# A masked copy of float64 bits in a compact tile, with its engine chosen by a list scheduler, and reordered first loads, in a one-core attention and feed-forward kernel

## The chip, the cores and the metric

One core of one Trainium2 chip. The metric is the device time of one execution in microseconds; lower is better. The kernel before has been run three times, and one further execution was taken with the profiler.

## What is computed

The inputs are float64 arrays for the weights and float32 for q, k, v. Three parts follow each other:

```python
kv  = einsum('bhsd,bhse->bhde', k, v)          # 8 batches, 8 heads, 576 rows, 64 wide
out = einsum('bhsd,bhde->bhse', q, kv)
x   = out / sqrt(mean(out * out, -1) + 1e-6) * g_norm      # then laid out as 4608 x 512
h   = maximum(maximum(x @ w1, x @ w2), x @ w3)             # 512 -> 768
x1  = h @ w_out                                            # 768 -> 512
g   = s * relu(x1 @ w_in) ** 2 + b                         # 512 -> 2048
y   = g @ w_out2                                           # 2048 -> 512
```

## The kernel before, in words

The rows are handled in nine blocks of 512 columns: one for each batch, and a ninth that gathers the 64 left-over rows of all eight batches. A product is kept near float32 accuracy by splitting each operand into a high and a low part and making three matmuls of 128x128 by 128x512 for each step (`mm3`, lines 154 to 157). The second feed-forward layer runs after all nine blocks, in stages that the change does not touch; only its weights are converted ("p" tiles, 32 of them) while the blocks are running.

**Weights.** They arrive as float64 bits and are turned into float32 on the core. `conv_load` (line 219) loads a tile of 128x512 numbers as 16-bit words, four to a number, into the slot that the finished weight will have (`W1S[n]` or `WOS[m]`). Then, in `plan_conv` (line 552): `conv_c` (line 235) clears the sign of the top word of each number and writes it into the fourth word of the same number, in place, that is at a step of 8 bytes; `conv_t` (line 253) makes the exponent and upper mantissa from it on ScalarE; `conv_r` (line 241) makes the low mantissa bits; `conv_s` (line 249) adds the sign; `conv_sum` (line 257) joins the two; `conv_hi` and `conv_lo` split the result. For the weights of the first layer ("w" tiles, 18, and "o" tiles, 6) `conv_c` runs on ScalarE, and `conv_r` on ScalarE for odd tiles and on VectorE for even ones; for "p" tiles both run on VectorE.

**Order of work.** Every step of the nine blocks is a `job` with a position, an engine, an estimated cost, and the names that it reads and writes. `arrange` (line 73) is a list scheduler: it simulates the engines with these costs and always starts the job that can begin first, among those on one engine the one with the lowest position. The order that comes out is then fixed for each engine: the engines run their instructions in that order, each waiting for what it needs, and nothing behind a waiting instruction on the same engine passes it. SyncE issues all loads and stores in this way (its queue is SPq in the rows).

**The start.** Positions count one per weight tile of 12 matmuls; a block takes 22 (`SL`), and the work ahead of block 0 begins at `Z = -12`. Batch 0: q is loaded, turned by TensorE and copied out; for each of four head pairs p, k and v are loaded, multiplied (`kv_mm`, line 322, including the left-over rows "rem"), copied (`kv_out`), and used (`o_mm`, line 389). For each two pairs a chain of small steps follows: copy out (line 409), square (415), mean over the heads by matmul (441), three ScalarE steps (451, 453, 455), two VectorE steps (457, 459), broadcast by matmul (470), scaling (475), and the split into xh (275) and xl (278). Call these chain 1 (pairs 0 and 1) and chain 2 (pairs 2 and 3). Weight tiles 0 to 3 are used pair by pair as they come: three matmuls for each tile and pair, 48 in all. From then on `g1_part` (line 509) makes 12 matmuls per tile, `g2_mm` (536) the 72 of the second product, while batch 1 goes through its attention (`plan_o`, `plan_norm`).

**Loads around the change.** Weight tiles 0 to 3 are loaded at positions `Z + LP[n]` with `LP = (3.35, 3.65, 3.95, 4.25)`, behind most of batch 0's q, k and v; the later tiles at `0.85 n - 5`, the "o" tiles at `10 + 0.8 m`; batch 2's k, v at 6, 9, 12, 15, its left-over rows at 6.01, its q at 12. The load of left-over rows of one batch has to wait until the products of the batch before have read the old ones. "o" tiles 4 and 5 share their slots with working tiles of the "w" conversions.

```python
def conv_c(key, eng):
    if eng == "ACT":
        act(out=mag16(key).bitcast(BF16), in_=top16(key).bitcast(BF16), func=AF.Abs)
    else:
        ts(out=mag16(key), in0=top16(key), scalar1=0x7FFF, scalar2=None, op0=ALU.bitwise_and)
```

## Time and profile before

| | us |
|---|---|
| three runs, median (lowest to highest) | 1410.27 (1410.04 to 1412.35) |
| the profiled execution, its own time | 1408.85 |
| its span, first to last instruction | 1406.8 |
| TensorE busy in the span | 1375.7 |
| VectorE busy | 909.9 |
| ScalarE busy | 750.5 |

The busy time of TensorE is the time in which at least one matmul was under way; matmuls overlap, so one that is shown with 0.39 us follows its neighbour after less. A row of the timeline gives the start, the duration, engine, line and shapes, and in brackets the idle time of the engine just before, with what ended it. In the rows, PE is TensorE, PEld its weight loads, DVE VectorE, ACT ScalarE, POOL GpSimd and SPq the queue of SyncE that issues transfers.

### The profile page before, as it was taken

The page shows a single profiled execution, that of the slowest core. Times are in us where ns is not written, and L with a number is a line of the kernel's source. Part 1 is how long each engine was busy: PE and PEld are TensorE (multiplying, and loading weights), DVE is VectorE, ACT ScalarE, POOL GpSimd, SP SyncE. Part 2 cuts the span into 40 slices and gives each one's busy share as a digit, 9 for nine tenths or more (in the row PEclk, how much of TensorE's full clock was granted, in tenths as well). Part 3 has the DMA queues.
Part 4 walks back from the last instruction along what each step waited for, and adds up shares of the span by engine and source line. Part 5 has one row for each costly group of instructions (what it writes and reads, how often), then busy time and mean ns, then how long its engine had stood idle before and what let it go on. Part 6 is the DMA issues. An engine that isn't in the chain of part 4 may idle for free. (4 is left out here: it accounts for less than half of the span.)

```text
span 1406.8 us, 19559 instructions
## 1 busy us (share of the span) xinstructions
PE 1375.7 (98%) x7056; PEld 1124.4 (80%) x7056; DVE 909.9 (65%) x1434; ACT 750.5 (53%) x1299; POOL 237.3 (17%) x175
## 2 busy tenths in 40 slices
PE   6999999999999999999999999999999999999997
PEld 3677888888888878888888789887888888888887
DVE  3886646465645462444648757467877978888884
ACT  6895434343424342333557456556775656566565
POOL 0000222221213132212000000000002314141412
PEclk9899999999999999999999999999999999999999
DMA  9976364445546320030354735544685454544441
GB/s 264 280 134 144 77 179 87 145 99 161 83 128 115 98 69 35 1 120 0 120 209 159 244 149 194 180 163 156 200 302 157 146 198 150 173 151 150 155 143 38
DMA packets 221328, 202.51 MB, mean 144 GB/s; under 512 B 117168, under 2 KB 175536, under 8 KB 219056
## 3 DMA queue, kind: packets, MB, share of 16 engines
q1 hardware_dynamic: 221072, 201.02, 48.0%
q8 instruction: 55, 0.90, 0.3%
q14 instruction: 41, 0.34, 0.1%
q10 hardware_dynamic: 160, 0.26, 0.0%
HBM read 126.79 MB, written 74.45 MB: 143 GB/s over the span
## 5 line engine op out<-in xcount | busy, mean ns | idle before, releaser
L155 PE MATMUL g<-xh,w_w 128*128 128x512 f32 x648 | 257.0, 397 | 4.1 <-ACT w_w L275 4.1
L157 PE MATMUL g<-xh,w_w 128*128 128x512 f32 x648 | 254.3, 393 | 0.2 <-DVE w_w L278 0.2
L156 PE MATMUL g<-xl,w_w 128*128 128x512 f32 x648 | 254.0, 392 | 0.0
L151 ACT ACTIVATE zx<-z 128x512 fp32r<-128x512 f32 (+1 forms) x280 | 161.2, 587 | 123.1 <-PE zs_a L963 34.0
L885 PE MATMUL ps_a<-x_q,w_q 128*128 128x512 f32 (+1 forms) x960 | 209.9, 370 | 3.5 <-DVE cs L793 3.2
L963 PE MATMUL zs_a<-zx,w_q 128*128 128x512 f32 (+1 forms) x960 | 203.8, 369 | 0.5 <-POOL zx L152 0.3
L885 PEld LDWEIGHTS ps_a<-x_q,w_q 128*128 128x128 f32 x960 | 167.4, 188 | 37.1 <-DVE cs L793 5.3
L152 DVE TENSOR_TENSOR zx<-z,zx 128x512 fp32r<-128x512 f32 (+1 forms) x234 | 172.5, 755 | 35.1 <-ACT zx L151 34.7
L963 PEld LDWEIGHTS zs_a<-zx,w_q 128*128 128x128 f32 x960 | 167.9, 188 | 32.0 <-POOL zx L152 0.7
L152 POOL TENSOR_TENSOR zx<-z,zx 128x512 fp32r<-128x512 f32 (+1 forms) x46 | 64.4, 1400 | 591.0 <-DMA gd<-cs 379.7
L527 DVE TENSOR_TENSOR h<-g,h 128x512 f32<-128x512 f32 x108 | 74.6, 691 | 115.4 <-PE g L157 114.0
L155 PEld LDWEIGHTS g<-xh,w_w 128*128 128x128 f32 x648 | 122.4, 189 | 33.1 <-ACT w_w L275 6.4
L157 PEld LDWEIGHTS g<-xh,w_w 128*128 128x128 f32 x648 | 122.5, 189 | 27.9 <-DVE w_w L278 2.0
L156 PEld LDWEIGHTS g<-xl,w_w 128*128 128x128 f32 x648 | 122.7, 189 | 25.3
L278 POOL TENSOR_TENSOR h<-h,h 128x512 fp32r<-128x512 f32 x40 | 54.7, 1367 | 464.2 <-ACT h L275 464.2
L885 PE MATMUL ps_b<-x_q,w_q 128*128 128x512 f32 (+1 forms) x480 | 106.4, 369 | 1.4 <-ACT cs L896 1.1
L963 PE MATMUL zs_b<-zx,w_q 128*128 128x512 f32 (+1 forms) x480 | 103.8, 371 | 1.9 <-DVE zx L152 1.9
L275 ACT ACTIVATE h<-h 128x512 fp32r<-128x512 f32 x54 | 34.1, 631 | 131.1 <-DVE h L527 130.6
L963 PEld LDWEIGHTS zs_b<-zx,w_q 128*128 128x128 f32 x480 | 83.9, 188 | 18.9 <-DVE zx L152 3.2
L885 PEld LDWEIGHTS ps_b<-x_q,w_q 128*128 128x128 f32 x480 | 83.9, 188 | 17.9 <-ACT cs L896 1.9
L155 PE MATMUL g<-h,w_o 128*128 128x512 f32 x216 | 84.7, 392 | 0.3 <-DVE h L527 0.3
L156 PE MATMUL g<-h,w_o 128*128 128x512 f32 x216 | 84.1, 389 | 0.0
(171 smaller groups left out, 2009.5 us busy)
## 6 DMA issues: line engine op xcount, KB each, us to landing
z<-gd SPq DMA_DIRECT2D x64, 512.0 KB
gd<-cs SPq DMA_DIRECT2D x96, 256.0 KB
z<-gd SPq DMA_DIRECT2D x48, 256.0 KB
x1d<-x SPq DMA_DIRECT2D x36, 256.0 KB
raw_w<-in_moe_w_dram SPq DMA_DIRECT2D x18, 511.0 KB
k<-in_k_dram SPq DMA_DIRECT2D x32, 256.0 KB
v<-in_v_dram SPq DMA_DIRECT2D x32, 256.0 KB
wd<-tr_p SPq DMA_DIRECT2D x32, 256.0 KB
```

The lines of the kernel that those rows point to most:

```text
L151: act(out=hi, in_=src, func=AF.Copy)
L152: eng.tensor_tensor(out=lo, in0=src, in1=hi.bitcast(F32), op=ALU.subtract)
L155: nc.tensor.matmul(ps, lhsT=w[:, 0, sl], rhs=xh, start=first, stop=False)
L156: nc.tensor.matmul(ps, lhsT=w[:, 0, sl], rhs=xl, start=False, stop=False)
L157: nc.tensor.matmul(ps, lhsT=w[:, 1, sl], rhs=xh, start=False, stop=last)
L275: act(out=out, in_=src, func=AF.Copy)
L278: eng.tensor_tensor(out=out, in0=src, in1=hi.bitcast(F32), op=ALU.subtract)
L527: nc.vector.tensor_tensor(out=st["h", m], in0=ps, in1=st["h", m], op=ALU.max)
L885: nc.tensor.matmul(ps, lhsT=w[:, a, c], rhs=x[:, b_], start=new and k == 0 and e == 0, stop=k == HK - 1 and e == 2, skip_group_check=True)
L963: nc.tensor.matmul(ps, lhsT=w[:, a, c], rhs=x[:, b_, :n], start=new and k_ == 0 and e == 0, stop=k_ == 3 and e == 2, skip_group_check=True)
```

## The change

A mask's result goes into a compact tile of its own ("gc", 128x512 16-bit numbers, two buffers) instead of back between the float64 words. The list scheduler can be given two engines for one job with a cost for each; it takes the one that can begin first, the cheaper one at a tie. `conv_c` and `conv_r` of all tiles are given so. Weight tile 0 is loaded ahead of everything else (`LP[0] = -1`), tiles 1 to 3 take the positions that 0 to 2 had. Batch 2's k, v, left-over rows and q are placed behind the "o" tiles (14.5 to 17). Some estimated costs of loads change. Batch 1's attention is placed one position earlier and its norm steps closer together. `WS_`, `WO_`, `KM`, `AS`, `K1`, `KS` and `QP` carry the values that stood in the code before.

```diff
-    SIZE = {"g": 4, "t": 2, "st": 2, "qt": 2, "o": 2, "kvc": 3, "k": NP, "v": NP}
+    SIZE = {"g": 4, "t": 2, "st": 2, "qt": 2, "o": 2, "kvc": 3, "k": NP, "v": NP, "cgc": 2}
...
     def job(pos, eng, cost, fn, *args, r=(), w=(), a=(), lag=None):
-        jobs.append((pos, len(jobs), eng, cost, fn, args, r, w, a, lag or (2.0 if eng == "SP" else 0.1)))
+        jobs.append((pos, len(jobs), eng, cost, fn, list(args), r, w, a, lag or (2.0 if eng == "SP" else 0.1)))
...
             if not need[n]:
-                heaps.setdefault(e[2], []).append(n)
+                for eng in e[2].split("/"):
+                    heaps.setdefault(eng, []).append(n)
...
     while any(heaps.values()):
             begin, eng = min((max(free.get(e, 0.0), min(ready[n] for n in h)), e) for e, h in heaps.items() if h)
             n = min(m for m in heaps[eng] if ready[m] <= begin)
-            heaps[eng].remove(n)
             cost = todo[n][3]
+            if "/" in todo[n][2]:
+                names = todo[n][2].split("/")
+                begin, cost, eng = min((max(free.get(e, 0.0), ready[n]), c, e) for e, c in zip(names, cost))
+                for e in names:
+                    heaps[e].remove(n)
+                todo[n][5].append(eng)
+            else:
+                heaps[eng].remove(n)
             if eng == "DVE" and begin < pool:
                 cost += 0.9
             free[eng] = begin + cost
...
-                    heaps.setdefault(todo[m][2], []).append(m)
+                    for e in todo[m][2].split("/"):
+                        heaps.setdefault(e, []).append(m)
...
-    def mag16(key):
-        return st["raw", key].rearrange("p (n f) -> p n f", f=4)[:, :, 3]
-
-    def conv_c(key, eng):
+    def conv_c(key, gc, eng):
+        st["gc", key] = gc()
         if eng == "ACT":
-            act(out=mag16(key).bitcast(BF16), in_=top16(key).bitcast(BF16), func=AF.Abs)
+            act(out=st["gc", key].bitcast(BF16), in_=top16(key).bitcast(BF16), func=AF.Abs)
         else:
-            ts(out=mag16(key), in0=top16(key), scalar1=0x7FFF, scalar2=None, op0=ALU.bitwise_and)
+            ts(out=st["gc", key], in0=top16(key), scalar1=0x7FFF, scalar2=None, op0=ALU.bitwise_and)
...
     def conv_r(key, eng):
-        t = st["tr", key]
+        t, st["r", key] = st["tr", key], eng
...
         t = st["tr", key] = tr()
-        act(out=t[:, 0], in_=mag16(key), func=AF.Relu, scale=float(2 ** 19), bias=lim[:, 0:1])
-
-    def conv_sum(key, eng):
+        act(out=t[:, 0], in_=st.pop(("gc", key)), func=AF.Relu, scale=float(2 ** 19), bias=lim[:, 0:1])
+
+    def conv_sum(key):
         t = st.pop(("tr", key))
-        if eng == "ACT":
+        if st.pop(("r", key)) == "ACT":
             stt(out=t[:, 0], in0=t[:, 1], scalar=2 ** 19 - 1, in1=t[:, 0], op0=ALU.bitwise_xor, op1=ALU.bitwise_or)
         else:
             nc.vector.tensor_tensor(out=t[:, 0], in0=t[:, 0], in1=t[:, 1], op=ALU.bitwise_or)
...
     def stage(tag, name, shape, dtype):
-        return lambda: (at_ if tag[0] == "c" else base).tile(shape, dtype, tag=tag, name=name)
+        return lambda: (at_ if tag[0] == "c" else base).tile(shape, dtype, tag=tag, name=name, bufs=SIZE.get(tag, 1))
...
-        eng = "DVE" if kk[0] == "p" else "ACT"
-        reng = "ACT" if kk[0] != "p" and QACT(key) else "DVE"
-        job(load, "SP", 2.23, conv_load, key, src, ra, w=[raw], a=[(a, raw)], lag=6.0 if kk[0] == "p" else 2.0)
-        job(pos, eng, 0.43 if eng == "DVE" else 0.63, conv_c, key, eng, r=[raw], w=[raw + ":c"])
-        job(pos, "ACT", 0.71, conv_t, key, tra, r=[raw + ":c"], w=[tr + ":t"], a=[(pr, tr)])
-        job(pos, reng, 0.43 if reng == "DVE" else 0.71, conv_r, key, reng, r=[raw], w=[tr + ":r"])
+        gc = f"gc_{kk}"
+        gca = stage("cgc", gc, [P, N], U16)
+        job(load, "SP", 1.95, conv_load, key, src, ra, w=[raw], a=[(a, raw)], lag=6.0 if kk[0] == "p" else 2.0)
+        job(pos, "DVE/ACT", (0.43, 0.66), conv_c, key, gca, r=[raw], w=[gc], a=[("cgc", gc)])
+        job(pos, "ACT", 0.71, conv_t, key, tra, r=[gc], w=[tr + ":t"], a=[(pr, tr)])
+        job(pos, "DVE/ACT", (0.43, 0.72), conv_r, key, r=[raw], w=[tr + ":r"])
         job(pos, "DVE", 0.69, conv_s, key, r=[raw], w=[tr + ":r"])
-        job(pos, "DVE", 0.69, conv_sum, key, reng, r=[tr + ":r"], w=[tr + ":t"])
+        job(pos, "DVE", 0.69, conv_sum, key, r=[tr + ":r"], w=[tr + ":t"])
         if store is None:
             job(pos, "ACT", 0.63, conv_hi, key, slot, r=[tr + ":t"], w=[f"W_{kk}:0"], a=[(slot, f"W_{kk}")])
             job(pos, "DVE", 0.69, conv_lo, key, r=[tr + ":t", f"W_{kk}:0"], w=[f"W_{kk}:1"])
...
         for p in range(NP):
-            job(load(p), "SP", 2.5, load_kv, bb, p, w=[f"k{bb}.{p}", f"v{bb}.{p}"],
+            job(load(p), "SP", 2.1, load_kv, bb, p, w=[f"k{bb}.{p}", f"v{bb}.{p}"],
...
         for p in range(NP):
-            job(load(p), "SP", 1.1, load_q_rows, bb, p, w=[f"qraw{bb}:{p}"] + ([f"qraw{bb}:{NP}"] if p == 0 else []),
+            job(load(p), "SP", 0.95, load_q_rows, bb, p, w=[f"qraw{bb}:{p}"] + ([f"qraw{bb}:{NP}"] if p == 0 else []),
...
     def plan_q(bb, p, n, pos):
-        job(pos, "SP", 1.26 * n, load_q, bb, p, n, w=[f"qraw{bb}:{i}" for i in range(p, p + n)],
+        job(pos, "SP", 2.1 * n, load_q, bb, p, n, w=[f"qraw{bb}:{i}" for i in range(p, p + n)],
...
@@ -686,9 +693,11 @@
         job(pos + 0.2, "SP", 1.1, x1_store, j, n, r=[f"x1.{j}.{n}"])
 
     PLAIN, ROWS, QP = 2, 1, 1
+    WS_, WO_ = 0.85, 12
+    KM, A1, AS = 0.5, 3, 6
+    K1, KS, K2 = -2, 1, 14.5
     SQ = ["sq", "sqh", "sql", "sqx"]
-    QACT = lambda key: key[1] % 2
-    CP, LP = 4, (3.35, 3.65, 3.95, 4.25)
+    CP, LP = 4, (-1, 3.35, 3.65, 3.95)
     WIDE = {0: 2, 1: 4}
     CUT = SL * B - 0.2
     Z = -12
@@ -708,9 +717,9 @@
     plan_rems(0, -1)
     sets = ["craw", "ctr", "o5", "o4"]
     for n in range(G1):
-        plan_conv(f"w{n}", w1_src(n), 0.85 * n - 3 if n > 3 else Z + CP + n, 0.85 * n - 5 if n > 3 else Z + LP[n], W1S[n], sets[n % 4], slot=W1S[n])
+        plan_conv(f"w{n}", w1_src(n), WS_ * n - 3 if n > 3 else Z + CP + n, WS_ * n - 5 if n > 3 else Z + LP[n], W1S[n], sets[n % 4], slot=W1S[n])
     for m in range(M1):
-        plan_conv(f"o{m}", [(0, P, W16[3][m * P:(m + 1) * P, :])], 12 + 0.8 * m, 10 + 0.8 * m,
+        plan_conv(f"o{m}", [(0, P, W16[3][m * P:(m + 1) * P, :])], WO_ + 0.8 * m, WO_ - 2 + 0.8 * m,
                   WOS[m], sets[m % 2], slot=WOS[m])
 
     for j in range(NB):
@@ -718,20 +727,20 @@
         if j + 1 < B:
             bb = j + 1
             if bb == 1:
-                plan_kv(bb, lambda p: -2 + p, lambda p: p + 0.5, NP)
+                plan_kv(bb, lambda p: K1 + KS * p, lambda p: KM + KS * p, NP)
             else:
-                plan_kv(bb, lambda p: t - 16 + 3 * p, lambda p: t - 0.8 + 0.001 * p, NP)
+                plan_kv(bb, lambda p: t - 16 + 3 * p if bb > 2 else K2 + 0.5 * p, lambda p: t - 0.8 + 0.001 * p, NP)
             if bb < ROWS:
                 plan_q_rows(bb, lambda p: QP + 0.1 * p, lambda p: 4.4 + 6 * (p // 2) + 1.3 * (p % 2) if p < NP else 4.35)
             else:
-                plan_q(bb, 0, NP, max(t - 10, 1))
+                plan_q(bb, 0, NP, t - 10 if bb > 2 else K2 + 2.5 if bb == 2 else QP)
             for u in range(NP // 2):
-                a = t + (6 if bb > 1 else 6) * u + (4 if bb == 1 else 0)
+                a = t + 6 * u if bb > 1 else A1 + AS * u
                 plan_o(bb, u, [2 * u, 2 * u + 1], lambda p: a + 0.4 + 1.3 * (p % 2), a + 3)
                 plan_oout(bb, u, a + 3.7)
                 for i in range(2):
                     p = 2 * u + i
-                    c, d = a + 3.9 + 2.9 * i, 0.9 if bb > 1 else 0.4
+                    c, d = a + 3.9 + (2.9 if bb > 1 else 0.5) * i, 0.9 if bb > 1 else 0.2
                     plan_norm(bb, p, c, d, max(t + G1 + 0.2 + 0.5 * p, c + 7 * d) if j else 20 + 0.1 * p, "POOL" if p < 3 and j else "DVE")
             plan_rems(bb, t + 13.3)
         elif j + 1 == B:
```

## Rows read from the trace of the kernel before

**Rows 1.** The profile's first line, and from its table of transfers the weight loads.

```profile
span 1406.8 us, 19559 instructions
raw_w<-in_moe_w_dram SPq DMA_DIRECT2D x18, 511.0 KB
```

**Rows 2.** Busy time by stretch: stretch, length, engines with counts, granted clock, DMA share, GB/s.

```profile
0.00:37.00 37.00, 22.73 (x235) 13.77 (x235) 13.02 (x38) 23.05 (x36) 1.63 (x8) 0.99 0.98 268
37.00:42.50 5.50, 5.50 (x30) 4.02 (x31) 5.08 (x10) 5.43 (x7) 0.00 (x0) 0.50 1.13 155
66.80:73.20 6.40, 4.56 (x13) 3.08 (x12) 4.71 (x9) 6.40 (x11) 0.00 (x0) 0.75 1.08 373
125.00:1406.80 1281.80, 1267.67 (x6340) 1047.11 (x6338) 824.61 (x1277) 652.53 (x1159) 235.71 (x167) 1.00 0.45 137
```

**Rows 3.** Timeline of TensorE, from the first product to the tenth weight tile.

```profile
13.18 0.34 PE L330 MATMUL kvor<-vrem,krem 128*64 128x64 f32 x4 [1.37 <-DMA vrem<-in_v_dram]
...
22.98 0.59 PE L399 MATMUL ops<-qh,kvc 64*64 64x512 f32 x2
...
27.97 0.50 PE L155 MATMUL g<-xh,w_w 128*128 128x512 f32 x1 [0.51 <-ACT w_w L275]
...
34.49 1.13 PE L470 MATMUL bc<-uc,spread 32*128 32x512 f32 x4 [3.71 <-DVE uc L459]
36.91 0.79 PE L155 MATMUL g<-xh,w_w 128*128 128x512 f32 x1 [1.28 <-ACT w_w L275]
...
39.75 0.80 PE L155 MATMUL g<-xh,w_w 128*128 128x512 f32 x1
...
42.48 0.52 PE L155 MATMUL g<-xh,w_w 128*128 128x512 f32 x1
...
68.99 0.50 PE L155 MATMUL g<-xh,w_w 128*128 128x512 f32 x1 [1.84 <-ACT w_w L275]
```

**Rows 4.** One piece of the chain of waits, late in the kernel.

```profile
1066.45 5.44 PE zs_a L963 x24
```

**Rows 5.** Timeline of ScalarE in the first 66 us.

```profile
22.35 1.33 ACT L237 ACTIVATE raw_w<-raw_w 128x512 bf16<-128x512 bf16 x1
...
24.39 1.00 ACT L409 ACTIVATE o<-ops 128x1024 f32<-128x1024 f32 x1
...
28.65 1.36 ACT L237 ACTIVATE raw_w<-raw_w 128x512 bf16<-128x512 bf16 x1
...
32.76 2.48 ACT L237 ACTIVATE raw_w<-raw_w 128x512 bf16<-128x512 bf16 x2
...
54.71 0.38 ACT L335 ACTIVATE kvc<-kvor 128x256 f32<-128x256 f32 x1 [1.82 <-PE kvor L330]
```

**Rows 6.** Groups by shape up to 118 us (last: 100 to 700): count, busy, mean ns.

```profile
L237 ACT ACTIVATE raw_w<-raw_w 128x512 bf16<-128x512 bf16 x18 | 24.1, 1369 | 0.0
L255 ACT ACTIVATE tr_w<-raw_w,lim 128x512 int32<-128x512 uint16 x18 | 13.5, 761 | 0.2
L275 ACT ACTIVATE w_w<-tr_w 128x512 fp32r<-128x512 f32 x18 | 11.4, 638 | 0.0
...
L247 DVE TENSOR_SCALAR tr_w<-raw_w 128x512 int32<-128x512 uint32 x9 | 3.8, 418 | 0.0
...
L239 DVE TENSOR_SCALAR raw_p<-raw_p 128x512 uint16<-128x512 uint16 x32 | 24.6, 768 | 21.2 <-DMA raw_p<-in_moe_w_out_dram 14.8 <-DMA raw_p<-in_moe_w_in_dram 6.4
```

**Rows 7.** Busy time by stretch again, for the rate of the loads.

```profile
0.00:10.00 10.00, 6.03 (x70) 5.69 (x72) 1.74 (x16) 2.96 (x5) 1.63 (x8) 1.00 0.70 190
```

**Rows 8.** Timeline of SyncE's queue, and what it waited for from 48 to 62 us.

```profile
54.70 0.60 SPq L313 DMA_DIRECT2D krem<-in_k_dram  x1
...
56.03 2.79 SPq L227 DMA_DIRECT2D raw_w<-in_moe_w_dram  x4
...
66.21 11.75 SPq L345 DMA_DIRECT2D qraw<-in_q_dram  x4
...
SPq L313 <- PE kvor L330: 4.3, 1, 4.3
```

## The prediction

> **What bounds it now.** I read the busy times by stretch first. From 125 us to the end TensorE is idle for 1281.80 - 1267.67 = 14.1 us in all [rows 2], so a change in the first block can return only what is lost before that. Lost there are 37.00 - 22.73 = 14.3 us of idle time up to 37 us, 1.84 us between 66.8 and 73.2 us, and the half clock: granted clock 0.50 (1.2 of 2.4 GHz) from 37 to 42.5 us, after TensorE had been busy for 22.73 of 37 us, and 0.75 on average in the second stretch, behind that 1.84 us wait [rows 2, 3]. At full clock a matmul of 512 columns takes 5.44 / 24 = 0.227 us [rows 4].
>
> The timeline of TensorE shows three phases [rows 3]. To 13.2 us it waits for loads (batch 0's left-over rows of v came last). From there to 39.75 us it waits for the small steps of chains 1 and 2 and for weight tiles: 0.51, 3.71 and 1.28 us are named waits, and when chain 2 gives its first x, at 39.75 us, only 9 of the 24 matmuls that need chain 1 alone are done (six with tile 0, three with tile 1). From 42.48 us on it runs without a gap, but for the wait at 68.99 us.
>
> What ended these waits late is ScalarE: its masks take 1.37 us each, where a plain split of as many elements takes 0.64 us, and 24 of them (18 "w", 6 "o") make 33 us [rows 6]. In its timeline they stand between the steps of the chains: one ahead of chain 2's copy at 24.39 us, one behind the logarithm at 28.65 us, two at 32.76 us ahead of chain 2's x [rows 5]. So the first block has two limits in turn, transfers up to 13 us and ScalarE's fixed order after that.
>
> **The change, part by part.** The sum is made against the profiled execution: 1408.85 us, with a span of 1406.8 and 2.05 us around it [rows 1]; it lies 1.42 us under the median of the three runs, 1410.27, to which I add the result.
>
> *Tile 0 first.* Its 511 KB [rows 1] now go ahead of q, k and v. The transfers are the limit from about 5 us on (DMA share 0.98 over the first 37 us [rows 2]), so everything up to the left-over rows moves later. By the rate of the first ten microseconds, 190 GB/s, this costs 2.7 us; by 373 GB/s, seen from 66.8 to 73.2 us, 1.4 us [rows 2, 7]; the mean of 37 us, 268 GB/s [rows 2], gives 1.9. I take **+1.9** (1.4 to 2.7). Tiles 1 to 3 come no later than before, since the same bytes are ahead of tile 3.
>
> *Tile 0's conversion leaves the chains.* It can now be done while ScalarE and VectorE wait for batch 0. Without its mask of 1.33 and its 0.76 us step [rows 5, 6] chain 2's copy can begin when its products are there, at 22.98 + 0.59 = 23.6 [rows 3] instead of 24.39 us: **-0.8** (0.4 to 0.8).
>
> *Cheaper masks in chain 2.* The trace has no mask with a compact output. From below: 0.64 us on ScalarE (the plain split) or 0.42 us on VectorE (the step that reads at 8 bytes and writes compactly); from above: 1.37 and 0.77 us, as in place now [rows 6]. I take 0.65 and 0.45, because the ScalarE step that reads the masked words at the same 8-byte step and writes compactly takes 0.76 us [rows 6]: reading so far apart is not what is slow. The Trainium skill ("SBUF — State Buffer", section on the DMA port swizzle) says of SBUF's 16-byte lines that accesses lose nothing as long as two fall in a line. An 8-byte step puts two in a line, so by that rule the compact tile would save nothing; the reads agree with it, the in-place masks can't be explained by it. That outcome is the second rival below. With 0.65 us the mask at 28.65 costs 0.7 less, the two at 32.76 us 1.2 less of which x of chain 2 is late by 1.0, and some of them go to VectorE: **-2.0** for chain 2 (-0.7, one mask alone, to -3.5, none left between its steps). Its first x then comes 1.9 - 0.8 - 2.0 = 0.9 us earlier, near 38.9 us.
>
> *More done before chain 2 arrives.* With tile 0's mask, step and split out of the way (1.33 + 0.76 + 0.64 = 2.7 us) and five masks shortened by 0.7, ScalarE gets some 6 us ahead by 40 us, so tiles 1 and 2 and perhaps 3 are ready. Of the 15 matmuls left over, I take 10 to move into the gap, 10 x 0.227 = **-2.3** (0 to -3.4).
>
> *Half clock.* From 39.75 to 42.48 us six matmuls took 2.73 us [rows 3], where 6 x 0.227 = 1.4 is the full pace. With the gap fuller the clock may stay up: **-1.0** (0 to -1.4).
>
> *The stall at 68.99 us.* It is 1.84 us of waiting for a weight's high part and 0.25 x 6.4 = 1.6 us of clock [rows 2, 3], together 3.4. Two things feed it: ScalarE stands 1.82 us at 54.71 us for batch 1's products with masks queued behind it [rows 5], and the queue of loads stands 4.3 us, with four weight tiles behind, because batch 2's left-over rows wait for batch 1's products [rows 8]. The second goes, since these rows now stand behind the "o" tiles; the first weighs less with masks cheaper. But TensorE is also earlier by then. I take **-2.5** (0 to -3.4).
>
> *Batch 2 behind wo.* What was queued behind its loads, weight tiles, gains; what is late next is batch 2. Its q takes SyncE's queue 11.75 us [rows 8], against 8.4 in the new plan (5.0 in the old), so its transposes may stand up to 3.4 us too early in VectorE's fixed order, with "o" tiles and the split of batch 1 behind them and TensorE behind those. From below: nothing, for in the old order q came far ahead of its use. **+1.0** (0 to 3.4).
>
> *At nothing:* batch 1's attention one position earlier (it is needed only by the next block; the cover is 15 weight tiles of matmuls); mask and low mantissa of the 32 "p" tiles on either engine (they lie in the stretch after 125 us, where TensorE's idle time is 1.1% [rows 2]; without that cover it would be 32 x 0.35 = 11 us less on VectorE).
>
> Sum: 1.9 - 0.8 - 2.0 - 2.3 - 1.0 - 2.5 + 1.0 = **-5.7 us**, 1403.15 for the profiled execution, **1404.6** as a median. All best ends together give -11.1 (1399.2), all worst ends +5.0 (1415.3).
>
> **Rivals.** *1. Transfers take ScalarE's place.* With share 0.98 for 37 us and 1.13 after [rows 2], tiles 1 to 3 may land too late for the earlier conversions. For it: the loads ahead of them are the same bytes. Against it: ScalarE's mask at 28.65 us ran behind other steps, and no wait of it for a load stands in the rows [rows 5]. Then the gap is not filled and the clock falls as before: 1.9 - 0.8 - 2.0 - 1.0 + 1.0 = -0.9, 1409.4.
>
> *2. The mask does not get cheaper.* The cost is that of 16-bit output, not of the step. Half the masks still move to VectorE, at 0.77 us. Then 1.9 - 0.8 - 1.1 (five matmuls moved) - 1.0 (of the stall) + 1.0 = 0.0, 1410.3. The new plan's 0.66 and 0.43 us would be as wrong as the old 0.63 was.
>
> *3. Slower: the late start is not given back.* The scheduler starts whatever can begin first, so a step of a weight tile can still slip between any two steps of chain 2, now on both engines, with a VectorE step of about 0.7 us between its two. Then +1.9 - 0.4 + 0.7, and TensorE, out of ready work for 2.2 us longer, pays the half clock for six more matmuls, +1.4: +3.6, 1413.9. It decides if the first matmul on chain 2's x comes after 41 us.
>
> *4. It does not do what it says.* "o" tiles 4 and 5 must wait for slots, and the scheduler then lets batch 2's q go ahead of them; only the rows' wait is gone. That takes some 1 us off the gain, 1405.6.
>
> **How the numbers follow.** Forecast 0.63, rival 1 0.11, rival 2 0.12, rival 3 0.12, rival 4 0.02. About 0.2%, 2.8 us, is what a measurement of this kernel can tell from no change. Faster: the forecast and rival 4, 0.65. Same: rivals 1 and 2, 0.23. Slower: rival 3, 0.12. The range goes from the sum's best end, 1399.0, to 1411.5, over rivals 1 and 2 and the milder part of rival 3; what is left out is most of rival 3 and a little below.
>
> **What would show it.** Right: masks near 0.65 us on ScalarE and 0.45 on VectorE; the left-over rows' product near 15 us instead of 13.18; tile 0 converted before 20 us; 15 or more matmuls of tiles 0 to 3 before chain 2's x, which comes near 39 us; no wait of over 1 us near 65 us; four weight loads no longer behind left-over rows. Wrong: masks still above 1 us, a clock of 0.5 for more than 5 us, or VectorE waiting for batch 2's q. The stretch behind the first block should be as before; a difference of over 2 us there would overturn the argument.

## The result, and the profile after

| | before | after |
|---|---|---|
| median, us (lowest to highest; four runs each) | 1410.71 (1410.04 to 1412.35) | 1398.1 (1397.3 to 1399.49) |
| ratio, 95% interval | | 0.991 (0.9893 to 0.9927) |
| the profiled execution, us | 1408.85 | 1398.18 |

The change gains 12.6 us, 0.9%. The forecast had the direction, with a gain of 6.1 us (5.7 in its sum), about half of what came; the time lies 0.9 us below its range.

The first line of the page, and its row of TensorE:

```profile
span 1396.3 us, 19558 instructions
PE 1370.8 (98%) x7056; PEld 1121.7 (80%) x7056; DVE 890.1 (64%) x1413; ACT 745.9 (53%) x1320; POOL 235.7 (17%) x175
```

The busy times by stretch, as in [rows 2]; the block ends earlier now, so the stretch behind it begins at 113 us:

```profile
0.00:37.00 37.00, 27.53 (x292) 17.89 (x293) 20.63 (x51) 25.10 (x43) 1.63 (x8) 1.00 0.99 278
37.00:42.50 5.50, 5.50 (x26) 4.28 (x24) 5.50 (x10) 5.15 (x9) 0.00 (x0) 1.00 1.19 134
66.80:73.20 6.40, 5.67 (x32) 3.48 (x32) 6.40 (x12) 6.40 (x12) 0.00 (x0) 1.00 0.33 90
113.00:1396.30 1283.30, 1267.99 (x6341) 1047.21 (x6339) 804.87 (x1251) 665.25 (x1183) 234.10 (x167) 1.00 0.45 137
```

And the one stretch of the kernel before that [rows 2] does not have and the account needs:

```profile
95.00:125.00 30.00, 29.17 (x178) 20.49 (x175) 24.68 (x40) 22.25 (x33) 0.00 (x0) 1.00 0.34 106
```

These lines account for the span, 1406.8 - 1396.3 = 10.5 us:

| where | before | after | gained | forecast |
|---|---|---|---|---|
| idle to 37 us | 37.00 - 22.73 = 14.27 | 37.00 - 27.53 = 9.47 | 4.8 | 3.2 (-1.9 + 0.8 + 2.0 + 2.3) |
| idle from there to the end of the block | 1.84 + 0.83 = 2.67 | 6.40 - 5.67 = 0.73 | 1.9 | with the next: 2.5 |
| busy time of the same 7056 matmuls (mostly the clock) | 1375.74 | 1370.80 | 4.9 | (1.0 + 2.5 - 1.0) |
| idle behind the block | 14.13 | 15.31 | -1.2 | 0 |

The sum is 10.4. The forecast's sum was against one execution, and that one was 1.9 us under the median of its kernel; after's is 0.1 above its own. That is nearly all of the rest of the 12.6.

What TensorE does where the waits of [rows 3] stood, from its timeline after:

```profile
12.48 0.34 PE L337 MATMUL kvor<-vrem,krem 128*64 128x64 f32 x4 [0.46 <-DMA vrem<-in_v_dram]
...
27.54 0.50 PE L164 MATMUL g<-xh,w_w 128*128 128x512 f32 x1
...
32.81 1.13 PE L477 MATMUL bc<-uc,spread 32*128 32x512 f32 x4
...
36.05 0.50 PE L166 MATMUL g<-xh,w_w 128*128 128x512 f32 x1 [0.72 <-DVE w_w L285]
...
37.09 0.40 PE L164 MATMUL g<-xh,w_w 128*128 128x512 f32 x1
...
68.70 0.65 PE L406 MATMUL ops<-qt,kvc 64*64 64x512 f32 x3 [0.73 <-DVE qt L393]
```

The product of the left-over rows comes at 12.48 us, not later than before (13.18); in a second profile of this kernel it comes at 14.46. The 3.71 us wait ahead of `bc<-uc` is gone: 18 matmuls stand between 27.54 us and it. All 24 that need chain 1 alone are done when chain 2's first x is used, at 37.09 us (9 of 24 at 39.75 us before), and the clock stays at 1.00. By 42.5 us 48 weight matmuls have begun (39 in the second profile), against 16. Tile 0 is ready early; VectorE's timeline, then ScalarE's:

```profile
4.89 0.43 DVE L246 TENSOR_SCALAR gc_w<-raw_w 128x512 uint16<-128x512 uint16 x1 [1.78 <-DMA raw_w<-in_moe_w_dram]
...
7.92 0.69 DVE L285 TENSOR_TENSOR w_w<-tr_w,w_w 128x512 fp32r<-128x512 f32 x1 [0.69 <-ACT w_w L282]
```

```profile
5.35 0.72 ACT L262 ACTIVATE tr_w<-gc_w,lim 128x512 int32<-128x512 uint16 x1 [3.33 <-DVE gc_w L246]
...
7.26 0.63 ACT L282 ACTIVATE w_w<-tr_w 128x512 fp32r<-128x512 f32 x1
```

It is complete at 7.92 + 0.69 = 8.6 us. The masks, by shape up to 110 us, as in [rows 6]:

```profile
L244 ACT ACTIVATE gc_w<-raw_w 128x512 bf16<-128x512 bf16 x11 | 7.2, 663 | 2.3 <-DMA raw_w<-in_moe_w_dram 2.3
...
L246 DVE TENSOR_SCALAR gc_w<-raw_w 128x512 uint16<-128x512 uint16 x7 | 2.9, 420 | 4.6 <-DMA raw_w<-in_moe_w_dram 4.6
```

They take 0.663 and 0.420 us instead of 1.369, and 7 of 18 went to VectorE. SyncE's queue now holds ten weight loads in a row, where [rows 8] had a 4.3 us wait ahead of four, and batch 2's q comes behind them:

```profile
41.59 12.97 SPq L236 DMA_DIRECT2D raw_w<-in_moe_w_dram  x10
```

What tile 0's load delayed was TensorE's first matmul, which needs batch 0's q. Before, then after:

```profile
3.41 1.58 PE L372 MATMUL qps<-ident,qraw 64*64 64x64 f32 x16 [3.41 <-DMA qraw<-in_q_dram]
```

```profile
5.22 1.64 PE L379 MATMUL qps<-ident,qraw 64*64 64x64 f32 x16 [5.22 <-DMA qraw<-in_q_dram]
```

It starts 1.8 us later, but the product of the left-over rows, which ends this phase, doesn't. Why is in the first stretches of both kernels; the last two columns are the DMA share and GB/s. Before:

```profile
0.00:2.50 2.50, 0.00 (x0) 0.00 (x0) 1.20 (x13) 1.28 (x1) 1.63 (x8) 1.00 0.04 9
2.50:5.00 2.50, 1.55 (x16) 1.21 (x16) 0.54 (x4) 0.00 (x0) 0.00 (x0) 1.00 0.69 184
```

After:

```profile
0.00:2.50 2.50, 0.00 (x0) 0.00 (x0) 1.20 (x13) 1.28 (x1) 1.63 (x8) 1.00 0.20 34
2.50:5.00 2.50, 0.00 (x0) 0.00 (x0) 0.65 (x5) 0.00 (x0) 0.00 (x0) 1.00 0.86 263
0.00:10.00 10.00, 4.69 (x56) 4.42 (x58) 4.63 (x21) 3.74 (x6) 1.63 (x8) 1.00 0.79 237
```

The DMA engines had little to do at first: 2.5 us x (34 + 263 - 9 - 184) = 260 KB more moved in the first 5 us, half of the tile, and 10 us x (237 - 190 [rows 7]) = 470 KB more in the first 10 us, nearly all of its 511.

### The profile page after: what moved, and what is told of

Read it like the earlier page. It is cut to its first block, busy times and chain, and to the rows that moved or that the text cites. A ratio compares the mean times of both kernels' runs of the same rounds, so it can differ in the third digit from the quotient of the medians.

```text
span 1396.3 us, 19558 instructions
## 1 busy us (share of the span) xinstructions
PE 1370.8 (98%) x7056; PEld 1121.7 (80%) x7056; DVE 890.1 (64%) x1413; ACT 745.9 (53%) x1320; POOL 235.7 (17%) x175
```

## The experiments

Two yardsticks are given for each run: the ratio to the kernel before, measured beside it (six runs or fewer), and the start of batch 2's first product in the one profile (the row `ops<-qt,kvc` behind 115 us), which marks the end of the first block. What follows that row is nearly the same work in all kernels, but took 1274.9 to 1281.1 us in the profiles below, so the marker tells better what the block did and the ratio what it is worth. A profile is one execution: b1's took 1410.59 us, the slowest of its six and 4.5 us above their median, so its marker is too late to stand for that kernel.

| run | ratio (95%) | marker, us |
|---|---|---|
| before | 1 | 130.26 |
| after | 0.991 (0.9893 to 0.9927) | 118.47 |
| after_again | 0.9914 (0.9896 to 0.9932) | 120.47 |
| b1_compact_only | 0.9946 (0.9933 to 0.9959) | 128.40 |
| b2_tile0_first_only | 0.996 (0.9948 to 0.9972) | 127.82 |
| b3_compact_and_tile0 | 0.9942 (0.9928 to 0.9956) | 123.61 |
| e2_in_place | 0.9935 (0.9924 to 0.9947) | 124.53 |
| e3_tile0_late | 0.9936 (0.992 to 0.9953) | 123.29 |
| e4_fixed_engines | 0.9912 (0.99 to 0.9924) | 120.22 |
| e5_batch2_early | 0.9929 (0.9914 to 0.9943) | 123.25 |
| e6_attention1_as_before | 0.9933 (0.9919 to 0.9948) | 123.07 |
| e7_costs_as_before | 0.9913 (0.9899 to 0.9927) | 122.02 |
| e8_two_tiles_first | 0.9935 (0.9921 to 0.9949) | 124.86 |
| e9_turns_early | 0.9889 (0.9874 to 0.9903) | 117.84 |
| e10b_batch2_early_turns_early | 0.9892 (0.9873 to 0.991) | 117.56 |
| e11_in_place_turns_early | 0.9938 (0.9924 to 0.9952) | 124.64 |
| e12_two_tiles_turns_early | 0.9898 (0.9883 to 0.9913) | 119.62 |
| e13_tile0_late_turns_early | 0.9953 (0.9938 to 0.9968) | 124.03 |
| e14_attention1_turns_early | 0.9905 (0.9889 to 0.9921) | 118.55 |

Two profiles of the same kernel after differ by 2.0 us at the marker (left-over rows' product at 12.48 and 14.46 us). The markers below are set against the earlier one, 118.47; against the other each is 2.0 us less late.

### One part undone

The masks back in place:

```diff
-        st["gc", key] = gc()
+        st["gc", key] = st["raw", key].rearrange("p (n f) -> p n f", f=4)[:, :, 3]
...
-        job(pos, "ACT", 0.71, conv_t, key, tra, r=[gc], w=[tr + ":t"], a=[(pr, tr)])
+        job(pos, "ACT", 0.71, conv_t, key, tra, r=[gc, raw], w=[tr + ":t"], a=[(pr, tr)])
```

> The kernel after, but the mask is written back between the float64 words as before; order of the planner's jobs and their costs stay as in the kernel after. Theory A (the cheap masks are the main gain: ScalarE's load set the first block): masks on ScalarE go back to about 1.36 us and on VectorE to 0.75, some 15 x 0.7 + 9 x 0.33 = 13 us more work up to 95 us, and 5 to 9 us of the 12.6 us gain go: 1403 to 1407. Theory B (tile 0 first is the main gain, the masks only fill idle time): at most 2 us lost, 1398 to 1400.

0.9935, a loss of 3.5 us, and a marker 6.1 us later. TensorE waits 3.1 us for a transpose of batch 1's q; what that means follows behind e8. Tile 0 where it was:

```diff
-    CP, LP = 4, (-1, 3.35, 3.65, 3.95)
+    CP, LP = 4, (3.35, 3.65, 3.95, 4.25)
```

> The kernel after, with the load positions of weight tiles 0 to 3 as before (3.35, 3.65, 3.95, 4.25). Theory A: 1 to 3 us lost, 1399 to 1401, since tile 0 is then converted between the steps of chains 1 and 2 with cheap masks. Theory B: 6 us or more lost, 1404 or above. The forecast's own term (a start 1.9 us later because of tile 0) would make this kernel's batch-0 products start earlier than in the kernel after; the trace after already shows them at 12.48 against 13.18 us, so I expect them near 13.2 us again.

0.9936, a marker 4.8 us later; TensorE waits 5.5 us for `bc<-uc` and has begun 24 weight matmuls by 42.5 us instead of 48. The left-over rows' product comes at 13.69 us, no earlier than after (12.48 and 14.46). The engines fixed by hand:

```diff
-        job(pos, "DVE/ACT", (0.43, 0.66), conv_c, key, gca, r=[raw], w=[gc], a=[("cgc", gc)])
+        eng = "DVE" if kk[0] == "p" else "ACT"
+        reng = "ACT" if kk[0] != "p" and key[1] % 2 else "DVE"
+        job(pos, eng, 0.43 if eng == "DVE" else 0.66, conv_c, key, gca, eng, r=[raw], w=[gc], a=[("cgc", gc)])
...
-        job(pos, "DVE/ACT", (0.43, 0.72), conv_r, key, r=[raw], w=[tr + ":r"])
+        job(pos, reng, 0.43 if reng == "DVE" else 0.72, conv_r, key, reng, r=[raw], w=[tr + ":r"])
```

> The kernel after, with mask and low mantissa on fixed engines as before (mask on ScalarE for w and o tiles, on VectorE for p tiles; low mantissa by the tile's parity), compact tile kept. ScalarE gets 9 masks of 0.66 us more. Theory A: a small loss, 0 to 2 us, 1398 to 1400. Rival (the free choice of the engine is a main part): 3 to 5 us lost, 1401 to 1403.

0.9912: the free choice of the engine, part of the change's name, returns nothing that these runs can tell. Batch 2's loads where they were:

```diff
-                plan_kv(bb, lambda p: t - 16 + 3 * p if bb > 2 else K2 + 0.5 * p, lambda p: t - 0.8 + 0.001 * p, NP)
+                plan_kv(bb, lambda p: t - 16 + 3 * p, lambda p: t - 0.8 + 0.001 * p, NP)
...
-                plan_q(bb, 0, NP, t - 10 if bb > 2 else K2 + 2.5 if bb == 2 else QP)
+                plan_q(bb, 0, NP, max(t - 10, 1))
```

> The kernel after, with batch 2's loads at their old positions (k and v at 6, 9, 12, 15, q at 12). Theory A: the queue of loads again stands behind batch 1's products with weight tiles 13 and on behind it, but TensorE is not waiting for these: 0 to 2 us lost, 1398 to 1400. Rival C (the queue's order made the stall at 69 us): a wait of TensorE of 1 to 3 us near 60 to 65 us comes back, with the half clock behind it, 3 to 5 us lost, 1401 to 1403.

0.9929, a marker 4.8 us later. But the wait is not one for a weight. From its list of TensorE's waits to 125 us:

```profile
PE ops L406 <- DVE qt L393: 3.0, 1, 3.0
```

and its VectorE timeline:

```profile
72.14 0.79 DVE L393 STREAM_TRANSPOSE qt<-qraw 128x576 f32<-128x576 f32 x1
```

In the kernel after, this transpose of batch 1's q starts at 67.88 us and the product that needs it is held up by 0.73 us. In e5 the planner has put it three places later in VectorE's order, behind more steps of weight tiles; TensorE waits 3.0 us for it, and the granted clock of 66.8 to 95 us falls to 0.94. Batch 1's attention and norm steps where they were:

```diff
-                a = t + 6 * u if bb > 1 else A1 + AS * u
+                a = t + 6 * u if bb > 1 else 4 + AS * u
...
-                    c, d = a + 3.9 + (2.9 if bb > 1 else 0.5) * i, 0.9 if bb > 1 else 0.2
+                    c, d = a + 3.9 + 2.9 * i, 0.9 if bb > 1 else 0.4
```

> The kernel after, with batch 1's attention and norm steps at their old positions (4 instead of 3, wider apart). Forecast of the record: nothing, within 1 us of the kernel after, near 0.991 of the kernel before. Theory G (what is left between tile 0 plus compact tile and the whole change, some 4 us, is the order of batch 1's steps): 2 us or more lost, 0.9925 or above, with a wait of TensorE for batch 1's products or q.

0.9933, with the same wait, 4.1 us. The old cost estimates of loads:

```diff
-        job(load, "SP", 1.95, conv_load, key, src, ra, w=[raw], a=[(a, raw)], lag=6.0 if kk[0] == "p" else 2.0)
+        job(load, "SP", 2.23, conv_load, key, src, ra, w=[raw], a=[(a, raw)], lag=6.0 if kk[0] == "p" else 2.0)
...
```

> The kernel after, with the planner's old costs of the loads (2.23, 2.5, 1.1, 1.26 per pair). Forecast of the record: nothing by itself. Theory H (the costs decide what the planner thinks has landed, and with it where steps stand in the fixed order): 2 us or more lost, 0.9925 or above, with a wait of VectorE or ScalarE for a load, or of TensorE for q's transposes, that the kernel after does not have.

0.9913: nothing by the ratio, though the marker is 3.6 us later in a profile with 1.6 us of the same wait. And tile 1 ahead of batch 0 as well, to see from where a first load costs something:

```diff
-    CP, LP = 4, (-1, 3.35, 3.65, 3.95)
+    CP, LP = 4, (-1, -0.99, 3.35, 3.65)
```

> The kernel after, with weight tiles 0 and 1 both ahead of q, k and v: the suspected price of a tile at the head of the queue, doubled. The forecast said 1.9 us of later start per tile. Theory I (tile 0 went into a time in which the queue was empty: 9 GB/s in the first 2.5 us before): the second tile finds no such time, the left-over rows' product comes at 14 to 15.5 us instead of 12.5 to 13.9, and the kernel is 1 to 2 us slower than the kernel after. Rival (the start is not bound by transfers at all): the product stays below 14 us and the time is that of the kernel after or better.

0.9935, and again the wait for batch 1's transposes, 4.0 us. So e2, e5, e6 and e8, four unlike edits, all end with TensorE waiting 3 to 4 us at one place. In e5, e6 and e8 the planner has put the last of these transposes 3, 9 and 8 places later in VectorE's order than in the kernel after, so their losses can't be read as the worth of the parts undone. e2 is another case. Its instructions stand in the same order as those of the kernel after, on every engine, through that kernel's first 110 us; the transpose starts at 72.30 us instead of 67.88 because the masks ahead of it take longer. Its loss is the masks' own.

The kernel after once more, beside the last two runs below:

> The kernel after once more, as the measure for the runs with early transposes (0.9889 of the kernel before). Expected: 0.991 again, between 0.990 and 0.992. If it is 0.9895 or below, the early transposes gained nothing that can be measured.

It repeated its ratio, 0.9914.

### The late transposes moved, and the parts undone again

One line places batch 1's last two transposes three positions earlier, on top of the kernel after:

```diff
-                plan_o(bb, u, [2 * u, 2 * u + 1], lambda p: a + 0.4 + 1.3 * (p % 2), a + 3)
+                plan_o(bb, u, [2 * u, 2 * u + 1], lambda p: a + 0.4 + 1.3 * (p % 2) - (3 if bb == u == 1 else 0), a + 3)
```

> The kernel after with batch 1's last two transposes three positions earlier in the plan, so that they stand earlier in VectorE's order. Theory J (that wait is the one loss that undoing other parts brings back): here it takes away only 0.7 us of wait, so 0 to 1 us faster than the kernel after, 0.990 to 0.991 of the kernel before, and no wait for the transposes. Rival: VectorE is full there, so the steps that now stand later (a low part of a weight) make TensorE wait instead, 1 us or more slower.

0.9889, 1396.87 us: the fastest kernel of this study, though its interval still meets that of the kernel after. The wait for `qt` is gone. The next runs are this kernel with e5's, e2's, e8's, e3's and e6's edits as well.

Batch 2 early (e5's edit):

> Batch 2's loads at their old positions as in e5, and batch 1's last two transposes three positions earlier. Theory J: e5's loss goes, 0.990 to 0.9915 of the kernel before, no wait for the transposes. Rival C (the queue of loads): 0.993 as in e5, with a wait of TensorE for a weight near 60 to 70 us.

0.9892, marker 117.56 against 117.84: the whole loss of e5 is gone. In this order the place of batch 2's loads is worth nothing that can be told. The run doesn't bring back the 4.3 us wait of [rows 8], though: here the queue doesn't wait for batch 1's products at all from 48 to 62 us. What that wait cost in the kernel before is answered by b1, below.

Masks in place (e2's edit):

> The mask written in place as in e2, and batch 1's last two transposes three positions earlier. Theory J: at most 1.5 us of e2's 3.5 us loss stays, 0.991 to 0.992, since ScalarE is then full but not waited for. Theory A (ScalarE's load itself): TensorE waits for a weight's high or low part instead, and 0.993 or more stays.

0.9938 against 0.9889, 0.0049 x 1412.54 = 6.9 us, and 6.8 us at the marker. Here the wait for `qt` is gone too, but others stand in its place and the loss stays. Its waits of TensorE to 125 us:

```profile
PE g L164 <- ACT h L532: 2.0, 1, 2.0
...
PE g L164 <- DVE o_rem L425: 1.5, 1, 1.5
PE g L164 <- ACT w_w L282: 1.0, 2, 0.6
```

and its busy times in the second half of the block:

```profile
66.80:95.00 28.20, 24.20 (x117) 17.54 (x116) 24.94 (x44) 28.20 (x43) 0.00 (x0) 1.00 0.75 151
```

against e9's in the same stretch:

```profile
66.80:95.00 28.20, 27.09 (x130) 19.32 (x129) 25.94 (x47) 23.81 (x42) 0.00 (x0) 1.00 0.88 158
```

ScalarE is busy for 28.20 of 28.20 us, against 23.81. That is a loss of work, not of order: e9 and e11 run the same instructions in the same order, on every engine, through the first 110 us of e9. About 1 us of the 6.8 at the marker may be the scatter of the start (left-over rows' product at 14.09 against 13.00 us).

Two tiles first (e8's edit):

> Weight tiles 0 and 1 first as in e8, and batch 1's last two transposes three positions earlier. Theory J with theory I: e8's loss falls to the later start alone, about 1 us, 0.9915. Rival (the second tile costs by itself): 0.993 as in e8.

0.9898, marker 1.8 us later: the second tile moves TensorE's first matmul by another 1.2 us (its first wait is 6.8 us against 5.6). The left-over rows' product is at 13.65 against 13.00 us, within what two profiles of one kernel differ by, and the loss is inside the intervals.

Tile 0 late (e3's edit):

> Tile 0 to 3 at their old load positions as in e3, and batch 1's last two transposes three positions earlier. e3 showed no wait for the transposes, its loss lay up to 42 us (24 matmuls of weight tiles begun by 42.5 us against 48, a clock of 0.95 in the first 37 us). Theory: the loss of e3 is tile 0's own price, so 0.9925 to 0.9935 stays, 5 us above e9. Rival: part of it was the order behind, 0.991 or less.

0.9953, 9.0 us by ratio, but 6.2 us at the marker; behind it this profile shows 1281.1 us, the most of all. Its timeline of TensorE at the end of chain 1:

```profile
26.75 1.79 PE L477 MATMUL bc<-uc,spread 32*128 32x512 f32 x4 [3.59 <-DVE uc L466]
...
31.85 0.80 PE L164 MATMUL g<-xh,w_w 128*128 128x512 f32 x1 [0.20 <-ACT xh L282]
```

and its busy times to 37 us, with the granted clock behind POOL's column at 0.91:

```profile
0.00:37.00 37.00, 24.87 (x252) 15.99 (x254) 14.69 (x41) 20.30 (x36) 1.63 (x8) 0.91 0.96 263
```

With tile 0 late the planner lets its steps in between those of chain 1, which then ends at 26.75 instead of 24.20 us (e9) or 23.82 (before): 2.6 to 2.9 us of the loss are an order that neither kernel has, if all of this delay reaches the marker, which was not tested. What is left, 3.3 to 3.6 us, is an estimate of the worth of tile 0's place; alone, on the kernel before, it gave 2.4 at the marker and 5.7 by ratio (b2, below).

Batch 1's old order (e6's edit):

> Batch 1's attention at its old positions as in e6, and its last two transposes three positions earlier. Theory J: e6's loss was the wait of 4.1 us for a transpose; without it 0.989 to 0.9905, and the old order costs nothing by itself. Rival: 0.992 or more stays, with a wait of TensorE for batch 1's products.

0.9905, marker 0.7 us later: with the transposes out of the way, no difference that can be told.

### One part alone, on the kernel before

The compact tile only, with the engines as before:

```diff
...
-    def conv_c(key, eng):
+    def conv_c(key, gc, eng):
+        st["gc", key] = gc()
...
-            act(out=mag16(key).bitcast(BF16), in_=top16(key).bitcast(BF16), func=AF.Abs)
+            act(out=st["gc", key].bitcast(BF16), in_=top16(key).bitcast(BF16), func=AF.Abs)
...
-        act(out=t[:, 0], in_=mag16(key), func=AF.Relu, scale=float(2 ** 19), bias=lim[:, 0:1])
+        act(out=t[:, 0], in_=st.pop(("gc", key)), func=AF.Relu, scale=float(2 ** 19), bias=lim[:, 0:1])
...
```

> The kernel before with nothing but the compact tile for the mask (old order of loads, old engines, old costs in the planner, which already had 0.63 us for a mask on ScalarE). Theory D (three parts of about equal size that add up: cheap masks 3 to 4 us, tile 0 first 3 to 4, batch 2 later 2 to 3): 3 to 4 us faster than the kernel before. Rival E (parts only pay together, since tile 0 between the steps of the two chains holds the gap open): under 1.5 us faster. Rival F (the masks were the whole and the other parts mend what the new order breaks): 7 us or more faster.

0.9946, a gain of 7.6 us, with a marker 1.9 us earlier in the late profile named above. The gap ahead of chain 2 stays empty (11 weight matmuls begun by 42.5 us), and the clock falls as before:

```profile
37.00:42.50 5.50, 4.55 (x27) 2.67 (x26) 4.88 (x8) 4.22 (x7) 0.00 (x0) 0.50 1.14 188
```

But the stall of the kernel before at 68.99 us is nearly gone, though the queue of loads now waits longer, 5.9 us instead of 4.3. From its list of the queue's waits from 48 to 62 us, and its timeline of TensorE:

```profile
SPq L311 <- PE kvor L328: 5.9, 1, 5.9
```

```profile
69.83 0.50 PE L155 MATMUL g<-xh,w_w 128*128 128x512 f32 x1 [0.30 <-ACT w_w L273]
...
70.98 0.50 PE L157 MATMUL g<-xh,w_w 128*128 128x512 f32 x1 [0.42 <-DVE w_w L276]
```

The clock from 66.8 to 73.2 us is 1.00 here. So that wait of the queue did not make the stall.

Tile 0 first only:

```diff
-    CP, LP = 4, (3.35, 3.65, 3.95, 4.25)
+    CP, LP = 4, (-1, 3.35, 3.65, 3.95)
```

> The kernel before with nothing but the load positions of weight tiles 0 to 3 of the kernel after (tile 0 first). Theory D: 3 to 4 us faster, the left-over rows' product at 12.5 to 14 us as in all runs so far (no later start), tile 0 converted before 12 us, masks still 1.36 us. Rival E: under 1.5 us faster. The forecast's term of 1.9 us later would show as a product near 15 us and a loss of up to 2 us.

0.996, marker 2.4 us earlier. Now there is a tile for the gap, but the next ones wait for ScalarE:

```profile
PE g L155 <- ACT w_w L275: 4.0, 3, 2.5
```

and the clock from 37 to 42.5 us is 0.53. Both of these edits together:

> The kernel before with both, compact tile and tile 0 first, and nothing else. Theory D: 6 to 8 us faster than the kernel before. Rival E: more than the sum of the two alone by 3 us or more. Rival F: no more than with the compact tile alone.

0.9942, marker 6.7 us earlier, 27 weight matmuls begun by 42.5 us, clock 0.73. At the marker the two together give more than 1.9 + 2.4 = 4.3 us; by ratio less (0.0058 against 0.0054 + 0.0040). With profiles that scatter by 2 us, and b1's far from its median, how they add is open. That 11, 20 and together 27 weight matmuls have begun by 42.5 us would fit that each part needs the other; but two profiles of the kernel after have 48 and 39, so this isn't shown.

From b3 to the kernel after there are still 0.0032, 4.5 us, and 5.1 at the marker, for the free engines, the two reorderings and the estimates together. Undone one by one (e4, e10b, e14, e7) none of them loses that much; which of them it takes together was not tried.

### The price of the mask by itself

Twelve extra masks at the start of the kernel after, on memory that is idle then, with distances of 8, 4 and 2 bytes between the 16-bit words written (s4 and d4 at 8 bytes, d2 at 4, d16 without gaps), and two with 32-bit words:

```diff
...
+    for out_, in_ in ((s4[:, :, 3], s4[:, :, 2]), (d4[:, :, 3], s4[:, :, 2]), (d2[:, :, 0], s4[:, :, 2]),
+                      (d16[:, :N], s4[:, :, 2]), (d4[:, :, 3], s16[:, :N])):
+        act(out=out_.bitcast(BF16), in_=in_.bitcast(BF16), func=AF.Abs)
+        ts(out=out_, in0=in_, scalar1=0x7FFF, scalar2=None, op0=ALU.bitwise_and)
+    act(out=s32[:, :, 1].bitcast(F32), in_=s32[:, :, 0].bitcast(F32), func=AF.Abs)
+    act(out=d32[:, :, 1].bitcast(F32), in_=s32[:, :, 0].bitcast(F32), func=AF.Abs)
```

> The kernel after with 12 small steps on an idle tile ahead of the work, to measure the mask by itself: in place at a step of 8 bytes; into another tile at 8 bytes; into another tile at 4 bytes; into another tile without gaps; from a tile without gaps to 8 bytes; the same on VectorE; and on ScalarE 32-bit words at 8 bytes in place and into another tile. If writing 16-bit words with gaps is what is slow: about 1.36 us on ScalarE and 0.75 on VectorE for every output with gaps, 0.66 and 0.42 without. If working in place is what is slow: 1.36 and 0.75 only in place. If it is the step of 8 bytes whatever the width: 32-bit words are slow as well.

This kernel was executed once. ScalarE's timeline, in the order of the code; the first row holds three masks that write with gaps:

```profile
3.38 3.07 ACT L226 ACTIVATE o_rem<-o_rem 128x512 bf16<-128x512 bf16 x3 [1.36 <-DVE o_rem L218]
...
7.70 0.68 ACT L226 ACTIVATE o_rem<-o_rem 128x512 bf16<-128x512 bf16 x1 [0.42 <-DVE o_rem L227]
...
9.48 1.35 ACT L226 ACTIVATE o_rem<-o_rem 128x512 bf16<-128x512 bf16 x1
...
11.66 0.65 ACT L228 ACTIVATE o_rem<-o_rem 128x512 f32<-128x512 f32 x1 [0.82 <-DVE o_rem L227]
12.22 0.64 ACT L229 ACTIVATE o_rem<-o_rem 128x512 f32<-128x512 f32 x1
```

Narrower windows give the three singly: in place at 8 bytes, into the other tile at 8 bytes, and into the other tile at 4 bytes.

```profile
3.38 1.34 ACT L226 ACTIVATE o_rem<-o_rem 128x512 bf16<-128x512 bf16 x1 [1.36 <-DVE o_rem L218]
...
4.46 1.40 ACT L226 ACTIVATE o_rem<-o_rem 128x512 bf16<-128x512 bf16 x1
...
5.61 0.84 ACT L226 ACTIVATE o_rem<-o_rem 128x512 bf16<-128x512 bf16 x1
```

Working in place is not what is slow: 1.34 us in place, 1.40 into the other tile. Reading at 8 bytes and writing without gaps takes 0.68 us; reading without gaps and writing at 8 bytes 1.35. In place or into another tile makes no difference for 32-bit words, and at that 8-byte step they take 0.65 and 0.64 us. So the price is that of writing 16-bit words far apart. VectorE has the same pair, without gaps and then at 8 bytes:

```profile
8.41 0.43 DVE L227 TENSOR_SCALAR o_rem<-o_rem 128x512 uint16<-128x512 uint16 x1
...
10.87 0.75 DVE L227 TENSOR_SCALAR o_rem<-o_rem 128x512 uint16<-128x512 uint16 x1 [1.04 <-ACT o_rem L226]
```

## Why the prediction was right or wrong

**What bounds it: right.** The first block, then ScalarE's place between the chains. In the stretch behind it the difference is 1.2 us of idle time, below the 2 us that the prediction had named as overturning the argument.

**Tile 0 first, +1.9: wrong.** The step priced the whole load at the mean rate of the loads and let "everything up to the left-over rows" move later by it. The first matmul did move, by 1.8 us; the left-over rows' product, which ends the phase, did not. It came at 12.48 us instead of the forecast 15 (14.46 in the second profile); with tile 0 late it came at 13.18 (before), 13.82 (b1), 13.69 (e3) and 12.95 (e13). The tile went out while the transfers were not yet the limit, in stretches of 9 and 184 GB/s that it raised to 34 and 263, and nearly all of its bytes were made up by 10 us. What a load costs where the queue is full, no run here shows: the second tile of e8 and e12 moved the first matmul again, but not this product beyond its scatter (13.57 and 13.65).

**Chains and gap, -0.8 - 2.0 - 2.3 = -5.1: about right.** Idle time to 37 us fell by 4.8. That is one number for three terms, so it bears out their sum and not each of them. Chain 2's x was used from 37.09 us on (forecast near 38.9), and all 15 left-over matmuls moved into the gap where 10 were forecast. The single parts suggest, in one profile each, that the terms are not separate: b1 has no tile ready and 11 matmuls by 42.5 us, b2 has one and waits 4.0 us for ScalarE.

**Half clock, -1.0: right in kind, mis-sized.** It priced six matmuls from 39.75 us on, though [rows 2] showed 0.50 over all of 37 to 42.5 us, 5.50 x 0.50 = 2.75 us. All of it came back (1.00 after), and busy time fell by 4.9 us in all: 2.75, the 1.6 of the later dip, and some 0.5 that no single stretch shows.

**The stall at 68.99 us, -2.5: right in size, wrong in one of its two causes.** 1.84 + 1.6 - 0.73 = 2.7 us came back. But the queue of loads, with its 4.3 us wait, had no part that shows: in b1 the queue waits 5.9 us, and with nothing but cheaper masks the stall falls to 0.30 and 0.42 us at full clock. ScalarE's masks had the part: b2, which keeps them in place, still waits 1.25 us there, and e11 fills ScalarE again.

**Batch 2 behind wo, +1.0: did not come.** The prediction asked which transposes would stand too early in VectorE's order, and named batch 2's; those that were late were batch 1's, by 0.73 us, because the planner had put the last of them late in VectorE's order (e9 moves it, and the wait is gone).

**At nothing: right** as far as the runs tell for the engines (e4), and for batch 1's order once its transposes are early (e14). In the change as it stands that order does matter: e6 loses some 3 us by ratio, because the planner then puts a transpose nine places later. The sum had no term for what the planner's order does.

**The rivals.** 1 fell: VectorE did wait 2.81 us for tile 1, until 19.71 us, but the tiles were ready for the gap (the one wait of TensorE left there is 0.72 us, on VectorE's low part). 2 fell: the masks' 0.663 and 0.420 us are within 0.03 of the 0.65 and 0.45 taken. Of the rule behind it, the Trainium skill ("SBUF — State Buffer", section on the DMA port swizzle) says that two accesses in a 16-byte line suffice for the full rate. The reads (0.68 us at an 8-byte step) and the 32-bit words (0.65) agree with that, the 16-bit writes at the same step (1.34 to 1.40) don't, and the measurement decides. 3 fell: the first matmul on chain 2's x came at 37.09, not after 41 us. 4 fell: the ten weight loads went ahead.

The steps that failed are thus three: the start moved late by the first load (+1.9, where nothing shows), the size of the half clock (-1.0, where 2.75 came back) and batch 2's late transposes (+1.0, which did not come). All three erred towards too small a gain. The sum lacks 10.4 - 5.7 = 4.7 us: 1.6 lie in the idle time to 37 us (the +1.9), 4.3 in clock and waits behind it (6.8 gained against 1.0 + 2.5 - 1.0, the clock's size and the +1.0 above all), and 1.2 were given back later. The range began at 1399.0, a little below the sum's best end of 1399.2, and the time lies below both.

## What to carry to other kernels

Price a load that is put first by what the queue moves in that moment, not by the mean rate, and by the wait that ends its phase, not by the first one; price a fallen clock over the whole stretch that the profile shows it in. Where a planner fixes the order, undoing a part can bring a wait somewhere else: before its loss is called the part's worth, compare the two orders and look up which wait ends last. Where the order has changed, take that wait out and undo the part again (e5 lost 2.7 us by ratio, e10b 0.4). Where it has not, the loss is the part's own (e2, e11). A busy engine that is off the path for most of the time still decides if gaps between dependent chains can be filled.

## What was not expected of the hardware

ScalarE took twice as long for 512 16-bit words written 8 bytes apart (1.34 to 1.40 us, against 0.68 without gaps; 0.84 at 4 bytes), and VectorE 0.75 against 0.43; 32-bit words at the same step ran at full pace (0.65 us).

A mean clock over a long stretch hides where the clock was low: e13 was busy for 24.87 of 37 us and had 0.91 there, the kernel before 22.73 and 0.99, because e13's half clock lay inside the 37 us and that of the kernel before behind them. In the rows the clock fell to 0.50 behind waits of TensorE: of 3.71 and 1.28 us before, of 3.59 us in e13, and of only 1.89 us in b3 (0.50 from 34 to 40 us). In e11 it stayed at 1.00 behind one of 2.03 us, so the length of one wait doesn't decide. In the kernel after, whose longest wait past 6 us was 0.82 us in the first block, it did not fall there.
